# Starting the joined matmul visits at head pair 4 instead of 6, in a linear-attention plus SoLU feed-forward kernel with a written-out instruction order

## The chip, the cores and the metric

The kernel runs on one core of one Trainium2 chip. The metric is the device time of one execution in microseconds (us). A core has five instruction streams that run side by side and meet only at semaphores: TensorE (PE in the profile, its weight loads PEld), VectorE (DVE), ScalarE (ACT), GpSimd (POOL) and SyncE (SP), which here issues every DMA. Each stream is worked off in its own order, so an instruction that waits holds up all that stand behind it on its engine.

## The reference

Attention with a feature map, for 8 batches of 8 heads, 576 tokens and head width 64, and then a feed-forward stage over the 4608 tokens:

```python
proj = x @ w_phi                                   # x is q or k, 64 -> 128
proj = proj - max(abs(proj), axis=-1)
phi  = concat([exp(proj), exp(-proj)])             # 256 features
kv   = k_phi^T @ v ;  z = sum over tokens of k_phi
num  = q_phi @ kv  ;  den = q_phi @ z + 1e-6
x    = num / den                                   # heads side by side: 4608 x 512
h    = x @ w_in                                    # 512 -> 1024
solu = h * softmax(h)
out  = (layernorm(solu) * g_ln) @ w_out            # 1024 -> 512
```

All inputs are float32 (the two big weights arrive as float64 bits and are converted on the chip).

## The kernel before, in words

**Attention.** Heads are handled in pairs. Head pair n (0 to 31) is sub-pair n % 2 of unit u = n // 2, and a unit is half of a batch. For a unit the keys are projected (`kp`, tile `pjk`), reduced to a row maximum (`km`) and subtracted (`ks`, tile `dk`) on VectorE, and exponentiated on ScalarE (`ke`, tile `ek`). The queries go one of two ways. Units 0 to 2 project them like the keys (`qp`, `pjq`; then `dq`), turn them on TensorE (`qT`, tile `dT`) and exponentiate them into the features `fq` (`qe`). From unit 3 on they go through a split into high and low parts (`qh`, `qlo`, tile `hq`), `pq`, VectorE turns (`blk`, `pT`) and two small TensorE turns (`mtp`, `mcp`).

**A visit** (`visit`, line 599; `V` in the plan) is the stretch of matmuls that makes the key-value sums of one pair in one PSUM bank: 10 matmuls `kvT<-ek,...` and then the sums z. For units 0 to 2 (`Z_PE`) the z sums are 20 small matmuls against `ones` and `ones_half`; from unit 3 on they are four matmuls on `zacc`, which GpSimd has added up before.

**From the bank to the query side.** For units 0 and 1 (`KV_PE`) the sums are copied by ScalarE (`kvs`), turned on TensorE (`kvt`) and copied again into `kvf`. From unit 2 on, VectorE turns them (`kve`, tile `kvs`), one DMA takes them to DRAM (`kvo`, `dk<-kvs`) and four DMAs bring them back as `kvf` (`kvi`, `kvf<-dk`). Then `q_num` (line 792) makes two `num` banks out of `fq` and `kvf`, and `q_den` (line 803) one `den` bank. ScalarE empties them (`qv`, `E<-num`; `de`, `dn<-den`), VectorE takes the reciprocal (`dc`, `cmr`), one DMA writes it to DRAM (`ds`, shown as `d<-cmr`), two bring it back over 64 partitions each (`db`, `rb<-d`), and GpSimd multiplies (`dv`, `xa<-E,rb`).

**Joined and separate.** In `visit`, if `before` is set, `q_num` of pair n - 1 stands ahead of pair n's `kvT` matmuls and `q_den` of pair n - 1 behind its z sums. `JOIN` (line 30) is the first pair whose visit does so. For smaller n, `num` and `den` of pair n - 1 are operations of their own (`qo`, `qd`), which may stand anywhere behind their inputs. A joined visit has to wait for the features `fq` and for `kvf` of pair n - 1 at its first matmul, and it takes all three PSUM banks of tag `a`.

**Feed-forward.** The 36 tiles of 128 tokens go through `moe_h` (24 matmuls into the bank pair `h`, of which there is one), a row maximum, exponential, product and turn, a trip through DRAM (`ub`, `du`, `uTs`), a split into `uhs` (ScalarE) and `uls` (GpSimd), and `moe_o` (24 matmuls). The first `moe_h` needs all of the first batch's `dv`, its split `mxh` (ScalarE) and `mxl` (GpSimd), and the four low parts `win_l` of `w_in` (GpSimd), each made from a `win_h` (ScalarE).

**What sets the order.** The function lists some 2620 operations with their engine, tiles and dependences. `SEQUENCE` (line 57) is a written-out order of their numbers, and `Plan.order` follows it: it gives each operation its buffers in that order and emits it, and each engine keeps that order. Every instruction is emitted through the helper `call` of `InOrder`, so all rows of the profile carry that helper's line, L271, and rows are told apart by their tiles.

Of the kernel before, what the change touches and what calls it, by code (L numbers as in the profile page):

```python
# [29 lines left out]
JOIN = 6  # L30
# [27 lines left out]
    99, 3, 2, 88, 0, 132, 126, 7, 136, 102, 4, 100, 101, 90, 103, 104, 5, 127, 107, 95, 89, 91, 230, 130, 14,  # L58
    186, 131, 96, 133, 92, 97, 145, 197, 128, 105, 137, 35, 106, 134, 53, 93, 129, 198, 98, 135, 199, 8, 140,
    109, 108, 138, 94, 148, 9, 142, 114, 149, 118, 143, 139, 146, 224, 147, 110, 115, 41, 10, 116, 150, 15, 111,  # L60
    231, 141, 144, 164, 295, 119, 16, 200, 234, 151, 232, 120, 201, 152, 188, 11, 121, 153, 165, 47, 154, 112,
    202, 187, 17, 113, 203, 156, 193, 36, 233, 155, 194, 166, 189, 157, 117, 225, 37, 158, 204, 18, 54, 170,
    167, 190, 122, 28, 12, 6, 38, 191, 13, 226, 192, 228, 169, 171, 42, 159, 227, 160, 235, 168, 205, 43, 172,
    296, 123, 39, 195, 328, 124, 196, 240, 44, 173, 216, 175, 241, 55, 48, 238, 161, 242, 229, 174, 162, 125,
    45, 29, 297, 285, 56, 246, 217, 243, 247, 218, 30, 248, 207, 245, 49, 244, 219, 31, 249, 46, 176, 50, 250,
    251, 178, 32, 252, 179, 40, 212, 163, 208, 19, 213, 253, 51, 254, 214, 177, 255, 59, 209, 215, 236, 256,
    329, 210, 239, 436, 206, 21, 284, 303, 180, 237, 52, 271, 338, 57, 334, 268, 286, 211, 60, 332, 269, 58,
    262, 287, 220, 257, 263, 437, 330, 61, 288, 264, 331, 22, 291, 270, 333, 272, 298, 438, 221, 181, 289, 62,
    292, 182, 273, 304, 290, 299, 258, 293, 300, 265, 23, 63, 222, 183, 344, 301, 305, 294, 67, 397, 302, 184,
    24, 33, 314, 520, 405, 223, 73, 345, 386, 85, 259, 74, 267, 76, 346, 266, 64, 25, 185, 274, 315, 306, 316,  # L70
    260, 310, 275, 34, 276, 398, 311, 307, 312, 335, 278, 317, 347, 308, 279, 439, 399, 75, 313, 339, 440, 280,
    277, 336, 318, 348, 20, 349, 337, 388, 319, 309, 340, 320, 350, 393, 321, 281, 351, 79, 68, 282, 261, 26,
    387, 389, 500, 352, 341, 394, 27, 390, 353, 441, 468, 354, 372, 442, 355, 511, 77, 342, 356, 283, 373, 395,
    374, 78, 358, 1871, 366, 359, 396, 443, 343, 357, 80, 444, 367, 322, 65, 445, 70, 1892, 446, 391, 82, 360,
    86, 361, 368, 469, 447, 362, 512, 71, 323, 1913, 1872, 81, 1873, 69, 87, 1874, 470, 83, 392, 324, 369, 1875,
    501, 400, 1893, 370, 550, 448, 371, 325, 401, 375, 1876, 449, 326, 1914, 402, 327, 407, 376, 1877, 377, 416,
    471, 408, 1915, 412, 472, 450, 409, 417, 413, 1880, 451, 473, 452, 477, 403, 475, 404, 66, 1916, 474, 1881,
    551, 476, 478, 418, 410, 411, 552, 422, 1917, 479, 1918, 1882, 1883, 1884, 1885, 519, 363, 453, 378, 1919,
    379, 1934, 72, 423, 1922, 1886, 424, 419, 480, 380, 553, 1894, 414, 481, 1923, 554, 364, 454, 425, 482,
    1920, 84, 406, 426, 555, 557, 1878, 427, 483, 1895, 484, 455, 428, 415, 1924, 1887, 457, 1925, 1926, 556,  # L80
    458, 420, 1927, 582, 459, 559, 1896, 1888, 456, 558, 1897, 421, 560, 381, 1898, 365, 382, 429, 1901, 485,
# [12 lines left out]
    1967, 747, 853, 739, 1968, 1969, 635, 608, 1970, 651, 1978, 636, 652, 1971, 637, 640, 638, 683, 641, 653,
    639, 685, 708, 654, 785, 642, 1979, 647, 2028, 709, 686, 684, 687, 643, 710, 1963, 783, 1980, 781, 1972,
    648, 782, 810, 740, 609, 784, 786, 711, 787, 649, 1973, 788, 789, 712, 1981, 713, 1982, 1985, 2029, 655,
    656, 728, 2030, 2031, 741, 2032, 610, 843, 657, 611, 714, 811, 812, 2033, 1986, 688, 612, 1983, 715, 956,
    1953, 2034, 689, 658, 717, 659, 730, 690, 1933, 613, 718, 1987, 742, 731, 2035, 735, 660, 2040, 732, 661,
    736, 662, 733, 743, 663, 734, 744, 1988, 716, 813, 758, 790, 1989, 815, 745, 2041, 892, 814, 737, 791, 816,
    1990, 2025, 738, 719, 792, 746, 759, 819, 793, 817, 2042, 818, 820, 760, 821, 794, 893, 924, 854, 748, 795,  # L100
    691, 1974, 764, 2043, 692, 894, 2044, 720, 693, 1991, 2026, 796, 2045, 722, 721, 723, 749, 799, 724, 694,
    897, 754, 925, 2036, 750, 755, 725, 765, 726, 2048, 1992, 926, 766, 895, 1993, 2049, 1954, 695, 896, 751,
    898, 767, 727, 901, 842, 822, 899, 1912, 823, 1994, 900, 855, 824, 2081, 902, 861, 752, 2082, 903, 768, 753,
    769, 756, 761, 2046, 797, 927, 904, 2083, 757, 800, 905, 928, 801, 906, 762, 798, 907, 825, 2084, 826, 908,
    763, 827, 2085, 2086, 2050, 770, 862, 2051, 2052, 2053, 771, 1984, 828, 2102, 2087, 2123, 2047, 829, 802,
    2054, 772, 803, 2090, 773, 804, 844, 805, 2091, 856, 845, 806, 957, 849, 774, 850, 775, 846, 1070, 857, 847,
    831, 830, 858, 851, 1995, 2124, 909, 2125, 2055, 929, 2126, 848, 852, 872, 832, 931, 2127, 2056, 833, 2088,
    2128, 2092, 776, 2093, 1081, 777, 873, 859, 930, 860, 933, 932, 2057, 2129, 874, 934, 2103, 910, 1006, 2094,
    807, 968, 2095, 1007, 878, 913, 2089, 2037, 2132, 911, 834, 1, 935, 2133, 1975, 835, 912, 1008, 2096, 879,
    880, 863, 836, 2134, 914, 967, 2104, 2058, 1038, 864, 2059, 865, 808, 868, 866, 2038, 881, 869, 867, 882,  # L110
    915, 837, 936, 1011, 1009, 883, 870, 2105, 1010, 884, 871, 1012, 1184, 937, 1997, 2135, 2136, 1013, 2106,
    1015, 2060, 2137, 838, 1014, 2107, 2097, 875, 938, 876, 939, 2098, 877, 1016, 1017, 940, 941, 885, 2130,
    1998, 942, 2138, 2108, 809, 1039, 2061, 916, 917, 1040, 958, 918, 970, 2062, 2139, 2111, 886, 2112, 2109,
    887, 839, 840, 963, 1195, 919, 888, 971, 964, 2113, 959, 889, 965, 972, 2114, 960, 1018, 973, 975, 2063,
    1071, 1019, 961, 945, 1020, 2115, 962, 1082, 943, 1083, 986, 890, 1021, 1047, 2116, 2064, 1041, 920, 2140,
    841, 2065, 944, 2066, 1022, 946, 1023, 2099, 966, 921, 974, 891, 947, 969, 987, 1120, 1042, 1090, 1045,
    1043, 2141, 1044, 1046, 988, 1024, 1048, 1025, 2131, 1049, 2100, 992, 2101, 1121, 2069, 1122, 2070, 2110,
# [1207 lines left out]
```

## Time and profile before

| | us |
|---|---|
| time, median of 3 runs | 709.77 (707.37 to 715.39) |
| the profiled execution, its own time | 708.93 |
| its span, first to last instruction | 707.1 |
| TensorE busy in the span | 694.5 |
| GpSimd busy | 512.3 |
| VectorE busy | 478.1 |
| ScalarE busy | 368.2 |
| first feed-forward matmul | 79.05 after the span's start |
| last matmul begins its operation | 700.00 |

The profiled execution's own time lies 1.8 us over its span, and 0.8 us under the median of the runs. Rows of the timeline give the start, the length, the engine, the line, the tiles written and read, and, in brackets, the idle time before the row and what ended it. On TensorE a row's length runs past the start of the next, since matmuls overlap: what an operation costs there is read from start to start. A float32 matmul leaves two records, so `x16` in a row stands for eight instructions. For DMAs the length is that of issuing on SP; the time to landing is listed apart.

### The profile page before, as it was taken

The page shows a single profiled execution, that of the slowest core. Times are in us where ns is not written, and L with a number is a line of the kernel's source. Part 1 is how long each engine was busy: PE and PEld are TensorE (multiplying, and loading weights), DVE is VectorE, ACT ScalarE, POOL GpSimd, SP SyncE. Part 2 cuts the span into 40 slices and gives each one's busy share as a digit, 9 for nine tenths or more (in the row PEclk, how much of TensorE's full clock was granted, in tenths as well). Part 3 has the DMA queues.
Part 4 walks back from the last instruction along what each step waited for, and adds up shares of the span by engine and source line. Part 5 has one row for each costly group of instructions (what it writes and reads, how often), then busy time and mean ns, then how long its engine had stood idle before and what let it go on. Part 6 is the DMA issues. An engine that isn't in the chain of part 4 may idle for free.

```text
span 707.1 us, 13443 instructions
## 1 busy us (share of the span) xinstructions
PE 694.5 (98%) x4894; PEld 520.2 (74%) x4894; DVE 478.1 (68%) x795; ACT 368.2 (52%) x684; POOL 512.3 (72%) x500
## 2 busy tenths in 40 slices
PE   8999999999999999999999999999999999999997
PEld 6666676777777777777777777777787777788886
DVE  6999787647867668577675777857567775354531
ACT  4997744626545564455554656535554554233231
POOL 1156999997878888789788997978868878361341
PEclk9999999999999999999999999999999999999999
DMA  8954465545575565566545555556374435320331
GB/s 293 339 191 120 114 199 163 157 115 161 162 214 151 143 201 151 166 167 193 144 116 162 188 164 156 173 164 191 107 201 156 127 109 149 94 94 24 124 116 67
DMA packets 113778, 110.04 MB, mean 156 GB/s; under 512 B 57648, under 2 KB 91184, under 8 KB 113200
## 3 DMA queue, kind: packets, MB, share of 16 engines
q1 hardware_dynamic: 113712, 109.18, 51.5%
q8 instruction: 39, 0.64, 0.4%
q14 instruction: 27, 0.22, 0.1%
HBM read 76.75 MB, written 32.39 MB: 154 GB/s over the span
## 4 chain that ended last, share of the span: by engine, by line
PE 64%; POOL 1%; DMA 1%; issue 1%; DVE 1%; ACT 0%; SPq 0%; ACTq 0%; POOLq 0%
PE h L271 22%; PE o L271 22%; PE kvT L271 6%; PE num L271 5%; PE pjk L271 3%; PE pq L271 3%; PE den L271 2%; DMA du<-ub 1%; DMA uTs<-du 0%; POOL xa L271 0%; PE uT L271 0%; PE mcp L271 0%; PE mtp L271 0%; POOL uls L271 0%; POOL zacc L271 0%
## 5 line engine op out<-in xcount | busy, mean ns | idle before, releaser
L271 ACT ACTIVATE ek<-dk 128x512 f32<-128x512 f32 (+1 forms) x160 | 87.2, 583 | 64.5 <-DVE dk L271 64.4
L271 PE MATMUL o<-w_out_h,uhs 128*128 128x512 f32 x264 | 105.3, 399 | 0.0
L271 PE MATMUL o<-w_out_h,uls 128*128 128x512 f32 x264 | 103.3, 391 | 0.1
L271 PE MATMUL o<-w_out_l,uhs 128*128 128x512 f32 x264 | 103.1, 390 | 0.0
L271 POOL TENSOR_TENSOR uls<-uTs,uhs 128x1024 fp32r<-128x1024 f32 x33 | 79.1, 2396 | 25.3 <-ACT uhs L271 22.9
L271 PE MATMUL h<-win_h,mxh 128*128 128x512 f32 x288 | 93.7, 406 | 0.0
L271 PE MATMUL h<-win_l,mxh 128*128 128x512 f32 x288 | 89.5, 392 | 0.0
L271 PE MATMUL h<-win_h,mxl 128*128 128x512 f32 x288 | 89.0, 390 | 0.0
L271 DVE TENSOR_REDUCE nm<-h 128x1 f32<-128x1024 f32 x36 | 43.7, 1215 | 64.5 <-PE h L271 64.4
L271 ACT ACTIVATE fq<-pT 128x576 f32<-128x576 f32 x104 | 68.4, 676 | 20.9 <-DVE pT L271 20.8
L271 POOL TENSOR_TENSOR zt<-ek 128x512 f32<-128x512 f32 x52 | 67.2, 1292 | 15.1 <-ACT ek L271 14.2
L271 POOL TENSOR_TENSOR hq<-rawq,hq 64x1152 fp32r<-64x1152 f32 x26 | 68.9, 2652 | 8.9 <-ACT hq L271 4.2
L271 PE MATMUL num<-fq,kvf 128*64 128x288 f32 x512 | 68.9, 412 | 0.8 <-DMA kvf<-dk 0.5
L271 ACT ACTIVATE eu<-h,nm 128x1024 f32<-128x1024 f32 x36 | 40.2, 1116 | 56.4 <-DVE nm L271 45.8
L271 DVE STREAM_TRANSPOSE blk<-pq 128x288 f32<-128x288 f32 x104 | 45.3, 459 | 28.2 <-PE pq L271 23.7
L271 DVE TENSOR_REDUCE m<-pjk 128x4 f32<-128x512 f32 (+1 forms) x80 | 48.5, 622 | 22.9 <-PE pjk L271 22.7
L271 PEld LDWEIGHTS h<-win_h,mxl 128*128 128x128 f32 x288 | 54.0, 188 | 12.1
L271 PEld LDWEIGHTS h<-win_l,mxh 128*128 128x128 f32 x288 | 54.0, 188 | 12.0
L271 PE MATMUL kvT<-ek,rawv 128*64 128x256 f32 x512 | 61.1, 380 | 0.0
L271 POOL TENSOR_TENSOR blk<-blk,mcol 128x1152 f32<-128x1152 f32 x26 | 55.4, 2131 | 5.7 <-PE h L271 3.5
L271 PEld LDWEIGHTS h<-win_h,mxh 128*128 128x128 f32 x288 | 50.7, 189 | 10.7 <-DVE kvs L271 0.5
L271 PEld LDWEIGHTS o<-w_out_h,uls 128*128 128x128 f32 x264 | 49.5, 188 | 11.5 <-POOL uls L271 0.7
(109 smaller groups left out, 1425.4 us busy)
## 6 DMA issues: line engine op xcount, KB each, us to landing
du<-ub SPq DMA_DIRECT2D x33, 512.0 KB, 2.9
uTs<-du SPq DMA_DIRECT2D x132, 128.0 KB, 3.1
rawq<-in_q SPq DMA_DIRECT2D x26, 576.0 KB, 4.6
rb<-d SPq DMA_DIRECT2D x64, 144.0 KB, 3.3
out<-os SPq DMA_DIRECT2D x35, 256.0 KB, 2.9
rawk<-in_k SPq DMA_DIRECT2D x32, 256.0 KB, 4.5
rawv<-in_v SPq DMA_DIRECT2D x32, 256.0 KB, 3.8
dk<-kvs SPq DMA_DIRECT2D x28, 192.0 KB, 1.9
```

What stands on the lines that cost most here:

```text
L271: return self.tc.keep_in_program_order(method(*args, **kwargs))
```

## The change

`JOIN` becomes 4. So the visits of pairs 4 and 5 (unit 2, sub-pairs 0 and 1) now carry `num` and `den` of pairs 3 and 4. Four operations vanish from the list (`qo` and `qd` of pairs 3 and 4), their 32 matmul instructions move into the two visits, no matmul is added or dropped, and all numbers behind them shift. `SEQUENCE` is a new order throughout, on all five engines. Its table is one line shorter, so the helper's line becomes L270.

```diff
-JOIN = 6
+JOIN = 4
 EARLY = (0, 1, 2)
...
 SEQUENCE = (
-    99, 3, 2, 88, 0, 132, 126, 7, 136, 102, 4, 100, 101, 90, 103, 104, 5, 127, 107, 95, 89, 91, 230, 130, 14,
...
```

Three places of the new order matter below.

TensorE, from the visit of pair 4 to the visit of pair 5. Before: the visit of pair 4, `num` and `den` of pair 3, projections and query turns, then the `kvT` of pair 5.

```order
L271 MATMUL kvT<-ek,ones_half 32x128 x4
L271 MATMUL num<-fq,kvf 64x288 x8
L271 MATMUL den<-fq,kvf 32x288 x8
L271 MATMUL pjq<-wph,rawq_764 128x256
L271 MATMUL dT<-ident,dq 128x128 x3
L271 MATMUL pq<-hq,w_hh 128x288
L271 MATMUL pq<-hq,w_l_76 128x288
L271 MATMUL pjq<-wph,rawq_761 128x128 x8
L271 MATMUL pjk<-wph,rawk 128x128 x8
L271 MATMUL dT<-ident,dq 128x128 x3
L271 MATMUL kvT<-ek,rawv 64x256 x8
```

And now: `den` of pair 3 closes the visit of pair 4, and `num` of pair 4 opens the visit of pair 5.

```order
L270 MATMUL kvT<-ek,ones_half 32x128 x4
L270 MATMUL den<-fq,kvf 32x288 x8
L270 MATMUL dT<-ident,dq 128x128 x3
L270 MATMUL pjq<-wph,rawq_661 128x256
L270 MATMUL pq<-hq,w_hh 128x288
L270 MATMUL pq<-hq,w_l_76 128x288
L270 MATMUL pjk<-wph,rawk 128x128 x8
L270 MATMUL dT<-ident,dq 128x128 x6
L270 MATMUL pjq<-wph,rawq_971 128x128 x8
L270 MATMUL num<-fq,kvf 64x288 x8
L270 MATMUL kvT<-ek,rawv 64x256 x8
```

The `num` of pair 4, which stood behind the `kvT` of pair 5 and more, has moved ahead of them; one more `dT` group stands between the visits, and little else.

SyncE, the round trip of pair 4's sums through DRAM. Before (`d_1041<-cmr` is the reciprocal of pair 3, `kvf<-dk` pair 4's sums coming back, `rb<-d_1041` pair 3's reciprocal coming back):

```order
L271 DMA rb<-d_871 64x2x288
L271 DMA dk<-kvs 128x384
L271 DMA rb<-d_871 64x2x288
L271 DMA vz_73<-in_v 64x128
L271 DMA kvf<-dk 32x12x32
L271 DMA vz_73<-in_v 64x128
L271 DMA d_1041<-cmr 128x9
L271 DMA kvf<-dk 32x12x32 x3
L271 DMA rb<-d_1041 64x2x288 x2
```

And now (`d_1026<-cmr` is that of pair 3):

```order
L270 DMA rb<-d_917 64x2x288
L270 DMA dk<-kvs 128x384
L270 DMA rb<-d_917 64x2x288
L270 DMA d_1026<-cmr 128x9
L270 DMA kvf<-dk 32x12x32 x4
L270 DMA rb<-d_1026 64x2x288 x2
```

All four loads of `kvf` now stand behind the DMA that waits for pair 3's reciprocal; before, one of them stood ahead of it.

ScalarE, from the copy `kvs` of pair 3 to the last features of pair 3. Before:

```order
L271 COPY kvs<-kvT 128x384
L271 ACTIVATE ek<-dk 128x4x128
L271 ACTIVATE fq<-dT 128x288
L271 ACTIVATE ek<-dk 128x4x128 x2
L271 COPY cms<-cmean 128x512
L271 ACTIVATE ek<-dk 128x2x128
L271 ACTIVATE ek<-dk 128x4x128
L271 ACTIVATE ek<-dk 128x2x128
L271 CAST win_h<-w_3_630 128x1024
L271 COPY kvf<-kvt 128x384
L271 ACTIVATE fq<-dT 128x288
L271 CAST w_out_h<-w_5_535 128x512
```

And now, with the last features of pair 3 in the last row:

```order
L270 COPY kvs<-kvT 128x384
L270 ACTIVATE ek<-dk 128x4x128
L270 ACTIVATE fq<-dT 128x288
L270 ACTIVATE ek<-dk 128x4x128
L270 ACTIVATE fq<-dT 128x288 x2
L270 COPY kvf<-kvt 128x384
L270 ACTIVATE ek<-dk 128x2x128
L270 COPY cms<-cmean 128x512
L270 ACTIVATE fq<-dT 128x288
L270 ACTIVATE ek<-dk 128x2x128
L270 ACTIVATE fq<-dT 128x288 x2
```

Before, the last features of pair 3 come in the row behind the last one shown, `fq` x3. Now two `ek` and the casts of `win_h` and `w_out_h` stand elsewhere.

272 rows, old and new, of the table SEQUENCE are left out of this document.

## The prediction

> **What bounds the kernel now.** I read the page first, then the busy times by stage, then TensorE's timeline around the two visits that change, and last the other engines there.
>
> ```profile
> PE 694.5 (98%) x4894; PEld 520.2 (74%) x4894; DVE 478.1 (68%) x795; ACT 368.2 (52%) x684; POOL 512.3 (72%) x500
> PEclk9999999999999999999999999999999999999999
> ```
>
> ```profile
> 20.00:58.45 38.45, 37.21 (x441) 24.55 (x440) 38.17 (x57) 36.96 (x77) 15.69 (x6) 1.00 0.67 226
> 69.00:79.05 10.05, 9.07 (x109) 5.72 (x108) 7.15 (x12) 7.26 (x17) 8.75 (x7) 1.00 0.57 163
> 79.05:120.00 40.95, 40.50 (x279) 29.55 (x278) 33.09 (x54) 22.68 (x44) 40.09 (x30) 1.00 0.52 148
> ```
>
> The columns are stage, length, then PE, PEld, DVE, ACT, POOL busy, clock, DMA share, GB/s. TensorE is the bound, at full clock, and its work is the same after the change. So the time can move only by what TensorE waits or loses between instructions. Up to 58 us VectorE (38.17 of 38.45) and ScalarE (36.96) are as full as TensorE; from 79 to 120 us GpSimd is (40.09 of 40.95). In these stages a delay is not made up easily. The stage that the change rebuilds lies between, from the visit of pair 4 (58.45) to the first feed-forward matmul (79.05). I call the start of pair 4's visit S. From the first feed-forward matmul on, both orders hold the same TensorE work, so what this matmul loses or gains on 79.05 is the forecast.
>
> **The visits themselves.** TensorE now, separate and joined:
>
> ```profile
> 58.45 1.95 PE L271 MATMUL kvT<-ek,rawv 128*64 128x256 f32 x16
> ...
> 60.76 1.08 PE L271 MATMUL kvT<-ek,ones 128*32 128x128 f32 x32
> ...
> 61.99 2.16 PE L271 MATMUL num<-fq,kvf 128*64 128x288 f32 x16
> 64.08 1.18 PE L271 MATMUL den<-fq,kvf 128*32 128x288 f32 x16
> 65.19 0.70 PE L271 MATMUL pjq<-wph,rawq 128*128 128x256 f32 x2
> ...
> 69.00 1.95 PE L271 MATMUL kvT<-ek,rawv 128*64 128x256 f32 x16
> ...
> 72.54 0.55 PE L271 MATMUL dT<-ident,dq 128*128 128x128 f32 x3
> 72.84 0.38 PE L271 MATMUL pq<-hq,w_hh 128*128 128x288 f32 x1
> ...
> 73.20 0.49 PE L271 MATMUL dT<-ident,dq 128*128 128x128 f32 x3
> 73.93 2.16 PE L271 MATMUL num<-fq,kvf 128*64 128x288 f32 x16 [0.25 <-DVE blk L271]
> ...
> 77.56 1.18 PE L271 MATMUL den<-fq,kvf 128*32 128x288 f32 x16 [0.73 <-ACT E L271]
> 78.67 0.41 PE L271 MATMUL pq<-hq,w_hh 128*128 128x288 f32 x1
> ```
>
> ```profile
> 95.18 2.16 PE L271 MATMUL num<-fq,kvf 128*64 128x288 f32 x16
> 97.17 1.90 PE L271 MATMUL kvT<-ek,rawv 128*64 128x256 f32 x16
> ...
> 99.43 0.42 PE L271 MATMUL kvT<-zacc,ones 128*32 128x128 f32 x8
> 99.67 1.15 PE L271 MATMUL den<-fq,kvf 128*32 128x288 f32 x16
> 100.76 0.29 PE L271 MATMUL mtp<-ident,m 128*36 128x128 f32 x1
> ```
>
> Start to start, separate: the visit 58.45 to 61.99 is 3.54, `num` to 64.08 is 2.09, `den` to 65.19 is 1.11, together 6.74. Joined, with the `ones` sums that these two visits keep: `num` 1.99 (95.18 to 97.17), `kvT` 2.26 (97.17 to 99.43), the sums 1.23 (60.76 to 61.99), `den` 1.09 (99.67 to 100.76), together 6.57. Joining saves 0.17 a visit, 0.34 for both. That is the whole direct gain, and it is contained in the absolute times below.
>
> **When pair 4's visit starts (S).** It now waits for pair 3's features. ScalarE before:
>
> ```profile
> 54.31 0.63 ACT L271 ACTIVATE ek<-dk 128x512 f32<-128x512 f32 x1
> 54.84 0.40 ACT L271 ACTIVATE fq<-dT 128x288 f32<-128x288 f32 x1
> ...
> 58.12 1.03 ACT L271 CAST win_h<-w 128x1024 fp32r<-128x1024 f32 x1
> 59.05 0.47 ACT L271 COPY kvf<-kvt 128x384 f32<-128x384 f32 x1
> ...
> 59.72 0.62 ACT L271 CAST w_out_h<-w 128x512 fp32r<-128x512 f32 x1
> 60.23 1.02 ACT L271 ACTIVATE fq<-dT 128x288 f32<-128x288 f32 x3
> ```
>
> The last features ended at 61.25 (60.23 + 1.02), 2.8 after S. The new order takes out from before them two `ek` (0.53 each, 54.31 to 54.84), the `win_h` cast (0.93) and the `w_out_h` cast (0.51), and adds one `fq` (0.30): 61.25 - 1.06 - 0.93 - 0.51 + 0.30 = 59.05. TensorE's own work ahead of S is unchanged, so 58.45 is the lower bound; if nothing of the regrouping helped, 61.25 is the upper. I take S = 59.05, since ScalarE is full up to there.
>
> **The new wait.** `num` of pair 4 had its place at 73.93; now it opens pair 5's visit, which thereby waits for pair 4's `kvf`. SyncE, VectorE and the landing of `kvf<-dk` (55 to 110 us, 12 of them) before:
>
> ```profile
> 67.79 0.33 SPq L271 DMA_DIRECT2D d<-cmr  x1
> 68.17 2.55 SPq L271 DMA_DIRECT2D kvf<-dk  x3
> 70.83 1.27 SPq L271 DMA_DIRECT2D rb<-d  x2
> ```
>
> ```profile
> 66.75 0.22 DVE L271 RECIPROCAL cmr<-dE 128x9 f32<-128x9 f32 x1
> ```
>
> ```profile
> DMA to landing us min/median/max: 2.3/2.9/4.3
> ```
>
> On SyncE all four loads of `kvf` now stand behind `d<-cmr` of pair 3, which waits for pair 3's reciprocal, and that for the `den` at the very end of pair 4's visit. The chain from S: the visit with `den` ends at S + 6.57. From the end of `den` to the end of the reciprocal it took 1.78 (65.19 to 66.97), so S + 8.35. Then `d<-cmr` is issued, 0.38 later the first `kvf<-dk` (67.79 to 68.17), and three more; one took between 0.64 (half of the 1.27 for two, the shape nearest to it) and 0.89 (68.17 to 70.83, three). The last is issued at S + 8.35 + 0.38 + 3 x 0.64 = S + 10.65 and lands 2.9 later: **S + 13.55**. The lower end is a landing of 2.3: S + 12.95. The upper end is the 0.82 that lay between reciprocal and `d<-cmr` before (another DMA stood there), 0.89 an issue and a landing of 4.3: S + 16.5.
>
> TensorE gets to the visit earlier. Between the visits stood 3.81 (65.19 to 69.00); one `dT` group is added, 0.30 (72.54 to 72.84): S + 6.57 + 4.11 = S + 10.7. So TensorE waits about **2.9** (2.3 to 5.8) in front of pair 5's visit, where before it waited 0.25 at `num` and 0.73 at `den`. Queued behind it on TensorE is all that leads to the feed-forward stage; queued on SyncE behind the `kvf` loads are the two `rb<-d` that the first `mxl` needs.
>
> Behind the visit stand three `pq` pairs (0.36 each, 72.84 to 73.20) and two `dT` groups (0.30), 1.7. The first feed-forward matmul then starts at S + 13.55 + 6.57 + 1.7 = S + 21.8 = 80.85 with S = 59.05. That is **1.8 later** than 79.05. Ends: S = 58.45 with the short landing gives 58.45 + 21.2 = 79.65, 0.6 later; S = 59.05 with the long chain 59.05 + 24.8 = 83.85, 4.8 later.
>
> GpSimd has to be ready there too:
>
> ```profile
> 71.48 2.36 POOL L271 TENSOR_TENSOR win_l<-w,win_h 128x1024 fp32r<-128x1024 f32 x1
> 75.15 1.41 POOL L271 TENSOR_TENSOR xa<-E,rb 128x576 f32<-128x576 f32 x1 [1.30 <-DMA rb<-d]
> ...
> 77.75 1.29 POOL L271 TENSOR_TENSOR mxl<-xa,mxh 128x512 fp32r<-128x512 f32 x1
> ```
>
> ```profile
> 76.59 0.62 ACT L271 CAST mxh<-xa 128x512 fp32r<-128x512 f32 x1 [0.84 <-POOL xa L271]
> ```
>
> The `rb<-d` pair is issued behind the `kvf` loads, from S + 11.3; from its first issue to `xa` it took 4.3 (70.83 to 75.15), so `xa` at S + 15.6. A `w_out_l` that filled the 1.2 between `xa` and `mxl` (76.56 to 77.75) stands elsewhere now, but `mxh` on ScalarE still needs its 0.62 there: `mxl` ends 1.41 + 0.7 + 1.29 = 3.4 later, at S + 19.0. In the new order the last `win_l` (2.36) stands behind this `mxl`, not ahead: S + 21.4, 0.4 under TensorE's S + 21.8. So this move costs nothing as long as the wait is there as estimated, and up to its own 2.36 if it is not.
>
> **The sum.** 708.93 (the profiled execution) + 1.8 = 710.7, the saving of 0.34 included. The median of the runs lies 0.84 above that execution, less than their spread of 8; I forecast 710.7.
>
> **The rivals.**
>
> A, *the later start is absorbed by GpSimd's pace*. From 79.05 to 120 GpSimd is at 40.09 of 40.95. If it sets the pace there, its own start counts: `mxl` ends at S + 19.0 = 78.05, 1.0 earlier than the 79.04 (77.75 + 1.29) of before, and then GpSimd has 2.36 more to do (`win_l`) and one `w_out_l` of 1.2 less, so it is 0.2 later in all: 709.1. Against it: TensorE has only 0.45 idle in that stage (40.50 of 40.95), so it can give back little.
>
> B, *the round trip is long* (the slower side). Place: pair 5's visit. Price: wait 5.8, 4.8 later, 713.7. It decides as soon as the last `kvf` lands after S + 13.55, and from there one for one, since nothing else is queued on TensorE that could run. For it: three loads took 2.66 before, and SyncE kept `d<-cmr` for 0.82. Against it: with four loads in a row nothing stands between them.
>
> C, *pair 3's features are not ready earlier*: S = 61.25, the first feed-forward matmul at 83.05, 4.0 later: 712.9. For it: VectorE and ScalarE are full until 58 us. Against it: the four instructions that left are measured.
>
> D, *the clock drops in the long wait*. At the start of the kernel TensorE is slow:
>
> ```profile
> 3.76 3.07 PE L271 MATMUL pjk<-wph,rawk 128*128 128x256 f32 x18
> ...
> 67.53 1.06 PE L271 MATMUL pjk<-wph,rawk 64*128 64x128 f32 x16
> ```
>
> ```profile
> PE pjq L271 <- issue: 1.7, 1, 1.7
> ```
>
> The 18 records took 3.07; the same work later takes little more than half (16 of them 1.06, and two wide ones 0.70 as in the `pjq` row at 65.19). It lasts to 6.8 (3.76 + 3.07); I take 5.6 of it for a second such stretch, as the first matmul of all began about 1 us into the span. If B's wait brought that state back for as long, half of 5.6 would be lost, 2.8: 716.5. The clock row shows full speed throughout, and TensorE's longest wait in this trace is the 1.7 of the row above, so it can't be seen here. The Trainium skill, "TensorE: Matmul & The Clock Gate", section "Part 1: The HAM clock gate", says that the clock is halved after an idle window of about 3.4 us and released after as long a busy one. By that rule the forecast's wait of 2.9 would cost no more than itself, and only B's would set it off; no run here shows that yet.
>
> E, *the new order loses less elsewhere*: TensorE idles 1.24 from 20 to 58.45 and 0.98 from 69 to 79.05, and the new order could fill both with pair 5's wait not showing either: 708.93 - 2.2 - 0.34 = 706.4.
>
> **How the numbers follow.** Forecast 0.50, A 0.20, B 0.12, C 0.08, D 0.04, E 0.06. About 1%, or 7 us, is what a measurement of this kernel tells from no change, since its runs spread by 8. All cases lie within 7 of 709.77. Only D with a late S, or B and C together, pass 716.9: slower by over 1% 0.08. For over 1% faster, TensorE would have to shed 7 us of waits, and the three stages above hold 2.7 of them (1.24, 0.98, 0.45): 0.04. Within 1%: 0.88. The forecast's own range is 709.5 (0.6 later) to 713.7 (4.8 later). The range over the cases reaches from E, less 1.9 for the runs' own scatter (2.4 below the median at the lowest), up to D: 704.5 to 716.5.
>
> **What would show it.** Right: `num` starts pair 5's visit with TensorE idle before it, 2 to 4 us, ended by the DMA `kvf<-dk`; the last `kvf` load issued some 10.7 after pair 4's visit began; the first `h` matmul near 80.9. `d<-cmr` stands idle on SyncE ahead of the loads, and pair 4's visit starts near 59. Wrong: no idle time ahead of pair 5's visit, or one that ends with `fq`; a first `h` before 79; a clock under 1 after it; or a changed idle sum behind 120 us that is larger than all of this.

## The result, and the profile after

The change takes 716.5 us (median of 20 runs, 711.3 to 720.9) where before takes 711.1 in the same session (20 runs, 706.1 to 715.4). The ratio is **1.0076, 95% interval 1.0054 to 1.0098**: slower by three quarters of a per cent, inside the bound of 1%, and 5.4 us where the forecast had 1.8. The profiled execution of the change took 714.81 with a span of 713.0, 5.9 more than before. Two rows of its page, TensorE's busy time and the granted clock:

```profile
PE 696.5 (98%) x4894; PEld 521.7 (73%) x4894; DVE 481.0 (67%) x795; ACT 369.8 (52%) x684; POOL 513.1 (72%) x500
PEclk9999899999999999999999999999999999999999
```

TensorE has the same 4894 records, and one slice of the clock row, the fifth, is no longer full. The three stages of the prediction, cut at this kernel's own marks (start of pair 4's visit, start of pair 5's visit, first feed-forward matmul):

```profile
20.00:61.02 41.02, 37.28 (x434) 24.44 (x432) 40.19 (x57) 37.23 (x81) 18.60 (x7) 1.00 0.62 222
76.01:85.83 9.82, 9.79 (x104) 6.30 (x104) 7.06 (x11) 4.59 (x9) 6.51 (x4) 0.86 0.22 84
85.83:120.00 34.17, 33.68 (x212) 25.03 (x214) 28.63 (x47) 20.07 (x41) 32.77 (x26) 1.00 0.60 179
```

Up to pair 4's visit TensorE is idle for 3.7 us (41.02 - 37.28), where it was 1.2; around pair 5's visit it has almost no idle time, but a clock of 0.86. TensorE's timeline shows where:

```profile
56.51 0.67 PE L270 MATMUL pjk<-wph,rawk 128*128 128x256 f32 x2 [2.13 <-issue]
...
61.02 2.16 PE L270 MATMUL num<-fq,kvf 128*64 128x288 f32 x16
...
67.47 0.55 PE L270 MATMUL dT<-ident,dq 128*128 128x128 f32 x3
...
70.65 0.33 PE L270 MATMUL dT<-ident,dq 128*128 128x128 f32 x1 [0.31 <-DVE dq L270]
72.07 0.87 PE L270 MATMUL dT<-ident,dq 128*128 128x128 f32 x3 [1.08 <-DVE dk L270]
72.87 2.08 PE L270 MATMUL pjq<-wph,rawq 64*128 64x128 f32 x16
76.01 3.49 PE L270 MATMUL num<-fq,kvf 128*64 128x288 f32 x16 [1.06 <-DMA kvf<-dk]
...
83.78 0.40 PE L270 MATMUL pq<-hq,w_hh 128*128 128x288 f32 x1
...
85.83 0.73 PE L270 MATMUL h<-win_h,mxh 128*128 128x512 f32 x2
```

The first `h` comes at 85.83, 6.8 later than the 79.05 of before; 0.9 of it is given back by the end. In order: 2.13 idle in front of `pjk`, so that pair 4's visit starts at 61.02 (S); a joined visit of 6.45 (61.02 to 67.47); three gaps of 0.31, 1.08 and 1.06; 16 `pjq` records in 2.08, and a `num` of 3.49 where the same 16 took 2.16 at 61.02. Three windows of 3.41, 6.83 and 3.41 us say why these two are slow:

```profile
68.50:71.91 3.41, 2.17 (x21) 1.48 (x19) 3.34 (x9) 2.76 (x7) 3.41 (x3) 1.00 0.30 77
71.91:78.74 6.83, 5.62 (x31) 3.94 (x33) 6.72 (x11) 1.11 (x4) 1.90 (x2) 0.50 0.71 197
78.74:82.15 3.41, 3.41 (x46) 2.27 (x46) 2.86 (x3) 2.27 (x5) 2.68 (x3) 1.00 0.02 6
```

The clock is exactly 0.50 from 71.91 to 78.74. The loads of pair 4's `kvf` on SyncE:

```profile
67.25 0.33 SPq L270 DMA_DIRECT2D dk<-kvs  x1
67.62 0.58 SPq L270 DMA_DIRECT2D rb<-d  x1
69.05 0.33 SPq L270 DMA_DIRECT2D d<-cmr  x1
69.49 2.64 SPq L270 DMA_DIRECT2D kvf<-dk  x4
```

The last of the four is issued at 71.50, S + 10.48, and lands 4.4 later; pair 5's visit starts at 76.01, S + 14.99. The row of `pjk` says `<-issue` for its 2.13 us: the profile shows nothing that ended them. I put them down to VectorE, which was late with everything behind the following instruction (its row, then GpSimd's up to 51 us and from there); the experiments test that:

```profile
48.58 3.44 DVE L270 SCALAR_TENSOR_TENSOR w<-wraw,w 128x1024 uint32<-128x1024 uint32 x1
```

```profile
48.56 2.37 POOL L270 TENSOR_TENSOR wsum<-wsum,w 128x1024 f32<-128x1024 f32 x1
...
51.01 3.25 POOL L270 TENSOR_TENSOR wsum<-wsum,w 128x1024 f32<-128x1024 f32 x1
```

I call this third bit step of `w`'s tile 0 **the bit step**. Alone it takes 1.22. Here it started 0.02 after a `wsum`, and ended at 52.02, 1.09 after that `wsum` ended (50.93): it did not run beside it, it waited for it. The next `wsum` in turn took 3.25 in place of 2.37.

### The profile page after: what moved, and what is told of

Same layout as the page of the kernel before. It is cut to its first block, busy times and chain, and to the rows that moved or that the text cites. A ratio compares the mean times of both kernels' runs of the same rounds, so it can differ in the third digit from the quotient of the medians.

```text
span 713.0 us, 13426 instructions
## 1 busy us (share of the span) xinstructions
PE 696.5 (98%) x4894; PEld 521.7 (73%) x4894; DVE 481.0 (67%) x795; ACT 369.8 (52%) x684; POOL 513.1 (72%) x500
## 4 chain that ended last, share of the span: by engine, by line
PE 80%; DVE 7%; DMA 5%; SPq 3%; issue 2%; ACT 2%; POOL 0%; ACTq 0%; DVEq 0%; POOLq 0%
PE h L270 26%; PE o L270 24%; PE kvT L270 9%; PE num L270 7%; PE pjk L270 5%; PE pq L270 3%; PE den L270 3%; SPq L270 3%; DVE w L270 2%; DVE m L270 2%; DMA uTs<-du 1%; DMA rawq<-in_q 1%; DVE dk L270 1%; DMA d<-cmr 1%; DVE eu L270 1%
## 5 line engine op out<-in xcount | busy, mean ns | idle before, releaser
L270 ACT ACTIVATE ek<-dk 128x512 f32<-128x512 f32 (+1 forms) x160 | 86.9, 582 | 51.9 <-DVE dk L270 51.8
L270 POOL TENSOR_TENSOR uls<-uTs,uhs 128x1024 fp32r<-128x1024 f32 x33 | 78.9, 2392 | 40.3 <-ACT uhs L270 35.6
L270 PE MATMUL o<-w_out_h,uhs 128*128 128x512 f32 x264 | 105.0, 398 | 0.0
L270 PE MATMUL o<-w_out_h,uls 128*128 128x512 f32 x264 | 103.2, 391 | 0.0
L270 PE MATMUL o<-w_out_l,uhs 128*128 128x512 f32 x264 | 103.1, 390 | 0.0
L270 PE MATMUL h<-win_h,mxh 128*128 128x512 f32 x288 | 94.0, 407 | 0.5 <-DVE eu L270 0.5
L270 PE MATMUL h<-win_l,mxh 128*128 128x512 f32 x288 | 89.5, 392 | 0.0
L270 PE MATMUL h<-win_h,mxl 128*128 128x512 f32 x288 | 89.1, 390 | 0.0
L270 POOL TENSOR_TENSOR zt<-ek 128x512 f32<-128x512 f32 x52 | 67.3, 1294 | 16.1 <-ACT ek L270 12.3
L270 ACT ACTIVATE fq<-pT 128x576 f32<-128x576 f32 x104 | 68.0, 678 | 17.7 <-DVE pT L270 16.8
L270 POOL TENSOR_TENSOR hq<-rawq,hq 64x1152 fp32r<-64x1152 f32 x26 | 69.0, 2655 | 8.6 <-ACT hq L270 3.2
L270 DVE TENSOR_REDUCE nm<-h 128x1 f32<-128x1024 f32 x36 | 43.6, 1210 | 44.8 <-PE h L270 44.6
L270 PE MATMUL num<-fq,kvf 128*64 128x288 f32 x512 | 70.6, 419 | 1.1 <-DMA kvf<-dk 1.1
L270 DVE STREAM_TRANSPOSE blk<-pq 128x288 f32<-128x288 f32 x104 | 45.1, 460 | 35.9 <-PE pq L270 32.3
L270 DVE TENSOR_REDUCE m<-pjk 128x4 f32<-128x512 f32 (+1 forms) x80 | 48.6, 620 | 28.0 <-PE pjk L270 27.9
L270 ACT ACTIVATE eu<-h,nm 128x1024 f32<-128x1024 f32 x36 | 40.2, 1117 | 46.2 <-DVE nm L270 42.2
L270 PEld LDWEIGHTS h<-win_h,mxl 128*128 128x128 f32 x288 | 54.1, 188 | 12.2
L270 PEld LDWEIGHTS h<-win_l,mxh 128*128 128x128 f32 x288 | 54.0, 188 | 12.1
L270 PE MATMUL kvT<-ek,rawv 128*64 128x256 f32 x512 | 60.9, 380 | 0.0
L270 PEld LDWEIGHTS h<-win_h,mxh 128*128 128x128 f32 x288 | 50.5, 189 | 11.2 <-issue 1.1
L270 DVE STREAM_TRANSPOSE pT<-blk 128x288 f32<-128x288 f32 x104 | 41.7, 444 | 24.3 <-POOL blk L270 21.1
L270 PEld LDWEIGHTS o<-w_out_h,uls 128*128 128x128 f32 x264 | 49.5, 188 | 11.0 <-POOL uls L270 0.2
```

What stands on the lines that cost most here:

```text
L270: return self.tc.keep_in_program_order(method(*args, **kwargs))
```

## The experiments

**The theory** after this reading has three causes: VectorE held up by GpSimd ahead of pair 4's visit (2.1 us), the round trip of `kvf` with what stands in its queue (the forecast's own), and the clock (1.3 us). **The rivals**: the time is the price of joining alone; or it is the price of the new order alone. Ratios below are to before on the same chip in the same session. Their intervals are some 0.2% wide on each side, so two kernels are told apart only from 0.3% on, about 2 us. Each kernel left one profile, and the same program can differ by 1.5 us from one profile to the next (the change's two, below), so a time read from a single trace is no finer than that.

### The loads ahead of `d<-cmr` (e1_loads_first)

```diff
 SyncE
-d<-cmr (pair 3)
 kvf<-dk (pair 4) x4
+d<-cmr (pair 3)
 rb<-d (pair 3) x2
```

> The change with one move: on SyncE d<-cmr of pair 3 stands behind the four kvf<-dk of pair 4 instead of ahead of them. Theory of the prediction (the loads queue behind d<-cmr, which waits for the end of den): the loads start as soon as kvf's own data are in DRAM. If that was much earlier, the wait in front of pair 5's visit shrinks by over 1 us. Rival (the round trip by itself is as long): dk<-kvs was issued at 67.25 and a load can't start before it has landed, about 2 us later, which is where the first load stood anyway (69.49); then pair 5's visit starts at most 0.4 us earlier (75.6 in place of 76.01) and the time falls by 0 to 0.4 us. I expect the rival: 716.1 to 716.5, clock still dropping to 0.5 near 72.

Ratio 1.0059 (1.0035 to 1.0082). SyncE, then TensorE:

```profile
68.32 0.33 SPq L269 DMA_DIRECT2D dk<-kvs  x1
68.69 0.58 SPq L269 DMA_DIRECT2D rb<-d  x1
70.22 2.63 SPq L269 DMA_DIRECT2D kvf<-dk  x4
```

```profile
75.96 2.37 PE L269 MATMUL num<-fq,kvf 128*64 128x288 f32 x16
...
84.62 0.40 PE L269 MATMUL pq<-hq,w_hh 128*128 128x288 f32 x1 [1.20 <-ACT dn L269]
```

The first load comes 1.90 after `dk<-kvs` where it came 2.24 after: standing behind `d<-cmr` cost 0.34, because the load could not start much earlier anyway. Two chains, over the reciprocal and over `dk`, end almost together. Pair 5's visit no longer waits (no load took 4.4 here) and starts at S + 13.87, 1.1 earlier where I expected at most 0.4; 1.20 turn up at once at a `pq` behind it.

### The bit step elsewhere (e2_w_later), three places later (e13_three_places)

```diff
 VectorE (e2; the load of raw tile 2 and its rescaling move behind it too)
-w<-wraw,w (tile 0, third step)
 m<-pjq (pair 4)
 ...
 cmr<-dE
+w<-wraw,w (tile 0, third step)
 w<-w,cms (wc 3)
```

> The change with the third bit step of w of tile 0 (the VectorE instruction that took 3.44 in place of 1.22 beside GpSimd's wsum) moved behind the second reciprocal, where GpSimd is idle; the load of raw tile 2 and its rescaling move behind it. Theory (VectorE was held up by GpSimd there, and all of VectorE behind it was late): it takes 1.22 again, wsum takes 2.4 both times, TensorE's 2.13 idle in front of pjk at 56.5 is gone, pair 4's visit starts at 58.6 to 59.4 in place of 61.02, the first h about 2 us earlier (83.5 to 84.3), and the time is 714.0 to 715.0. Rival (pair 3's features are late because ScalarE is full, whatever VectorE does): the visit starts at 60.5 or later, time 716 to 716.5.

```diff
 VectorE (e13; the load of raw tile 2 moves behind it too)
-w<-wraw,w (tile 0, third step)
 m<-pjq
 m<-pjk
 m<-pjq
+w<-wraw,w (tile 0, third step)
```

> The change with one thing alone: the bit step of w stands three places later on VectorE (behind two row maxima more and the one of pair 4's q), with the load that waits for it. Theory (a two-operand VectorE instruction that starts while GpSimd's wsum runs waits for the end of that wsum, and no longer): it starts at about 50.6, 0.3 before the wsum ends, and takes 1.2 to 1.6 in place of 3.44; TensorE's idle of 2.1 in front of pjk is under 0.6; pair 4's visit starts 1.6 to 2.3 earlier against (2,qp,0), the time falls by 1 to 2.6 us. Rival (the instruction is slow beside GpSimd wherever it stands): it takes over 2.5, time unchanged.

e2: ratio 1.0040 (1.0018 to 1.0061). TensorE's idle in front of `pjk` is gone, and pair 4's visit starts 11.30 behind the start of the first `pjq` of pairs 4 and 5 in place of 13.57, 2.27 earlier. But the bit step still took 2.75, now beside a `win_l`; and behind pair 5's visit a new idle stands. VectorE, GpSimd and TensorE of e2:

```profile
58.20 2.75 DVE L269 SCALAR_TENSOR_TENSOR w<-wraw,w 128x1024 uint32<-128x1024 uint32 x1
...
78.31 4.56 DVE L269 TENSOR_TENSOR w<-w,cms 128x512 f32<-128x512 f32 x2
```

```profile
57.51 2.36 POOL L269 TENSOR_TENSOR win_l<-w,win_h 128x1024 fp32r<-128x1024 f32 x1
...
78.04 1.50 POOL L269 TENSOR_TENSOR mxl<-xa,mxh 128x512 fp32r<-128x512 f32 x1 [0.73 <-ACT mxh L269]
79.58 2.73 POOL L269 TENSOR_TENSOR win_l<-w,win_h 128x1024 fp32r<-128x1024 f32 x1
```

```profile
83.92 1.54 PE L269 MATMUL dT<-ident,dq 128*128 128x128 f32 x6 [2.51 <-DVE blk L269]
```

The bit step ends at 60.95, 1.08 after the `win_l` (59.87). The two centrings of `w_out` (`w<-w,cms`, its column mean subtracted), 0.68 each alone, took 4.56 beside `mxl` and the next `win_l`, and the row subtraction and the `blk` in front of this `dT` stand behind them. The first `h` came at 85.11, but this whole trace runs 1.3 us later than the change's before the two orders part. Counted from the start of pair 3's visit (50.29 in the change, 51.60 here), it came after 33.5 in place of 35.5: 2.0 earlier. The ratio, 0.36% lower than the change's, says the same, 2.5 us, just over what can be told apart.

e13: ratio 1.0091 (1.0057 to 1.0124). The bit step started at 50.70, and the next `wsum` had started at 50.57:

```profile
50.70 3.32 DVE L269 SCALAR_TENSOR_TENSOR w<-wraw,w 128x1024 uint32<-128x1024 uint32 x1
```

```profile
50.57 2.37 POOL L269 TENSOR_TENSOR wsum<-wsum,w 128x1024 f32<-128x1024 f32 x1
```

My 1.2 to 1.6 missed, since I had not counted on the next `wsum` standing right behind. It ends 1.08 after that one (52.94), as an instruction does that waits for the other. The length of 3.32 alone would not tell this from a fixed slowness. What does is another bit step, some 30 us later, which started beside an `xa` in e3, e4, e5, e11, e13 and e14: it took anything from 1.42 to 2.32, and always ended 1.08 to 1.09 after that `xa`. The idle in front of `pjk` was 2.77, and nothing was gained.

### TensorE kept busy in the gaps (e3_keep_busy)

```diff
+def keep_busy(n):
+    t = bank("kv", [P, 512], "keep")
+    for _ in range(n):
+        nc.tensor.matmul(t[:, :P], lhsT=ident, rhs=ident, start=True, stop=True)
 TensorE
 pjk (pair 6)
+keep_busy(1)
 dT (pair 4)
+keep_busy(5)
 dT (pair 4)
 pjq (pair 5)
+keep_busy(5)
 the visit of pair 5
```

> The change with 11 matmuls more on TensorE, whose results nobody reads: 1, 5 and 5 of 128x128 on the identity, put where TensorE idled 0.31, 1.08 and 1.06 us between pair 4's and pair 5's visits. The wait for kvf stays. Theory (those gaps made the clock drop to 0.5 from 71.9 to 78.7, which cost pair 5's visit 7.77 - 6.45 = 1.3): the granted clock stays 1.00, the visit takes 6.45, the first h comes about 1.3 earlier (84.5), time 715.0 to 715.4. Rival (the clock drops for another reason, such as the small matmuls of the visits): clock 0.5 again, time as the change, 716.5 to 717.

Ratio 1.0056 (1.0028 to 1.0083), 0.20% or 1.4 us under the change, as expected, though the interval does not resolve it alone. Its windows from the gaps to the end of pair 5's visit, and TensorE behind it:

```profile
68.90:77.03 8.13, 8.09 (x83) 6.47 (x75) 7.71 (x15) 4.73 (x11) 5.09 (x4) 1.00 0.36 89
77.03:83.55 6.52, 6.52 (x94) 4.07 (x93) 6.52 (x7) 2.68 (x5) 3.59 (x3) 1.00 0.57 166
```

```profile
87.20 0.91 PE L269 MATMUL dT<-ident,dq 128*128 128x128 f32 x6 [2.59 <-DVE blk L269]
```

The clock stays full there and the visit takes 6.45, so it was the gaps that lowered it in the change. They don't always: the same two gaps stand in e2 and e13, where the clock stayed full. And this profile is not free of half clock either, with 3.41 us of it at 9.61, at 57.40 (behind the 2.12 idle in front of `pjk`) and at 88.12 (behind the 2.59 shown here).

The runs give an estimate of the price. From a run's mean clock and span follows, rounded, how many times 3.41 us it ran at half clock, (1 - clock) x span / (0.5 x 3.41). Of the 34 runs of before that stood beside e1 to e4, 2 had none (mean 708.4), 10 one (709.7) and 22 two (711.1): about 1.35 us each. Seven of the experiments' profiles show one or two of them between 9 and 18 us, far ahead of the visits. The change had two to four in 19 of 20 runs, 2.7 in the mean of these; the twentieth, 720.9 us, had a mean clock of 0.943. e3 had 1.8. The profiled execution of before, on which the forecast stood, was one with none.

### Joined and apart (e4_pair5_apart, e5_both_apart, e6_old_order)

```diff
-joined = n >= JOIN
+joined = n >= JOIN and n not in (5,)
 ...
-joined = JOIN <= n + 1 < 4 * B
+joined = JOIN <= n + 1 < 4 * B and n + 1 not in (5,)
 TensorE
 the visit of pair 5
+num, den (pair 4)
```

> The new order with only pair 4's visit joined: pair 5's key-value sums stand alone in the same place, and pair 4's numerators and denominators behind them. Theory (joining pair 5's visit put 3.5 us of sums that need no kvf behind the wait for kvf): the sums start when TensorE gets there, 74 to 75, num starts near 77.6 without a wait over 0.3, den ends near 80.8 in place of 83.8, the clock stays 1.00, the first h starts when mxl is there (82.2 to 82.8), 3 us earlier than in the change; time 713.2 to 714.0. Rival (GpSimd, which sets the pace from 79 to 120 us, takes the gain back): first h earlier, but the time stays within 1 us of the change, 715.5 to 716.5.

e5 has (4, 5) there, and pair 3's `num` and `den` behind pair 4's visit.

> The new order without either of the two new joins: pair 4's and pair 5's key-value sums stand alone where their joined visits stood, with the numerators and denominators of the pair before right behind. Rival of the prediction (the new order itself is what costs, by VectorE instructions that stall beside GpSimd's, and joining is nearly free): the time stays within 1 us of the change with pair 5 apart, 712 to 713.5, with TensorE's idle before pjk near 56 and the late first h (85 or later) both still there. The prediction's theory (the wait that joining adds is the price): 2 to 3 us faster than the change with one join, 709.5 to 710.5.

```diff
 TensorE, in the order of before
-kvT (pair 4's visit)
-num, den (pair 3)
+num (pair 3), kvT (pair 4), den (pair 3): one visit
 ...
-kvT (pair 5's visit)
 ...
-num, then den (pair 4)
+num (pair 4), kvT (pair 5), den (pair 4): one visit
+dT (pair 5, moved from ahead of it)
 ScalarE, in the order of before
+ek, E<-num (pair 4)
 fq (pair 5)
-ek
 fq (pair 5)
-E<-num (pair 4)
```

> The order of before with the two joins put into it: pair 4's visit moves to where pair 3's numerators stood, pair 5's to where pair 4's numerators stood, with one turn of pair 5's q behind it; nothing else is moved. Theory of the prediction (a joined visit waits for the features and for kvf): pair 4's visit waits for pair 3's features and starts near 61.3 in place of 58.45, the kvf chain of pair 4 ends some 13.5 after that, 74.8, and the first h comes at about 83, 4 later than before: 713.5 to 715. Rival (joining is nearly free, the order costs): within 1.5 us of before, 709.5 to 712.

e4: 1.0034 (1.0011 to 1.0057). e5: 1.0041 (1.0012 to 1.0071). e6: 1.0138 (1.0110 to 1.0165). Without any new join the new order is still slower than before, with an interval that excludes no difference: **about half of the loss, 0.41 of 0.76%, is there without joining**. Taking one or both joins out of it gains 0.35 to 0.42%, just about what can be told apart. That is not a clean price of the joins. e5's profile, as shown below, is also without the stall of the bit step, and e2, which has both joins and no idle in front of `pjk`, stands at 1.0040, where e5 stands. Neither rival holds alone. In e6 two instructions moved on ScalarE as well (diff above). It lost 9.8 us where I expected 4 to 5: in its trace pair 4's visit waits 1.06 for pair 3's `kvf` and, in the middle of its `num`, 1.03 for `fq`, and 1.75 and 2.32 follow ahead of a `pjq` and a `dT`. In e4's trace the sums started near the expected 74 to 75:

```profile
75.10 2.94 PE L269 MATMUL kvT<-ek,rawv 128*64 128x256 f32 x16
...
79.63 2.16 PE L269 MATMUL num<-fq,kvf 128*64 128x288 f32 x16
```

But they did not fill a wait: the last `kvf` load, issued at 72.36, had landed at 74.65, before they began. So what e4 gains is not that wait. The clock had dropped here too (2.94 for what takes 1.90), and the first `h` came at 85.41, not at 82.2 to 82.8. What settles the bit step is e5, where it and the `wsum` stand as in the change:

```profile
48.74 1.22 DVE L269 SCALAR_TENSOR_TENSOR w<-wraw,w 128x1024 uint32<-128x1024 uint32 x1
```

```profile
48.72 3.46 POOL L269 TENSOR_TENSOR wsum<-wsum,w 128x1024 f32<-128x1024 f32 x1
```

```profile
54.44 0.67 PE L269 MATMUL pjk<-wph,rawk 128*128 128x256 f32 x2
...
58.95 1.30 PE L269 MATMUL kvT<-ek,rawv 128*64 128x256 f32 x10
```

```profile
58.28 0.75 ACT L269 ACTIVATE fq<-dT 128x288 f32<-128x288 f32 x2
```

The same two instructions, started within 0.02 us of each other, went the other way: the `wsum` waited (3.46), the bit step took 1.22, TensorE has no idle in front of `pjk`, pair 4's visit starts at 58.95, and pair 3's features end at 59.03 (58.28 + 0.75) in place of 61.10. All traces of the new order agree. Counted from the start of pair 3's visit, pair 4's starts after 8.45 to 8.50 in the six without that idle (e2, e5, e9, e10, e11, e12), joined or apart. With it, it starts after 10.70 to 10.73 (e1 and the change), 11.36 (e13), and 12.27 to 12.37 (e3, e4, e14), where the idle time fell into one of the 3.41 us stretches and the next one ran at half clock. The Trainium skill, "SBUF — State Buffer", section "Who interferes with whom", says that a VectorE instruction with two inputs in SBUF and a GpSimd instruction that reads SBUF exclude each other, and that the one issued first blocks the other until it has finished. The traces agree that they exclude each other: in nine of them (change, e1, e2, e3, e4, e9, e10, e13, e14) the bit step ended 1.08 to 1.09 after the GpSimd instruction that was ahead of it. Which of the two was issued first they do not show: by its row the `wsum` starts 0.02 ahead in the change and in e5 alike.

### The change again (e14_change_again)

> The change once more, unchanged, beside the others on the same chip. If the stall of the bit step is decided by which of two instructions starts first (wsum at 48.56, the bit step at 48.58), either 3.4 or 1.2 may stand in this profile; if it is 1.2, TensorE's idle in front of pjk is gone with it. The landing of the last kvf load, 4.4 in the first profile, should be 2.3 to 3.2 as in the other kernels, and then pair 5's visit does not wait for it. Time 715.5 to 717.5 where before is at 711.

Ratio 1.0076 again (1.0045 to 1.0108). TensorE:

```profile
74.07 0.52 PE L270 MATMUL dT<-ident,dq 128*128 128x128 f32 x3 [1.08 <-DVE dk L270]
...
76.14 3.26 PE L270 MATMUL num<-fq,kvf 128*64 128x288 f32 x16
...
86.82 0.91 PE L270 MATMUL dT<-ident,dq 128*128 128x128 f32 x6 [2.00 <-DVE blk L270]
```

The stall of the bit step is there again (3.42), and the 1.08 in front of `dT`. The wait for `kvf` is not: the last load, issued at 73.50, landed 2.2 later, at 75.73. The 1.06 of the first profile was one slow landing (4.4). Pair 5's visit starts at S + 13.13. S itself is 1.5 later than in the first profile, counted from pair 3's visit: the clock was at 0.50 from 57.92 to 61.33, behind the idle time in front of `pjk`, where in the first profile it stayed full.

### Moves together (e9_three_moves, e10_three_moves_apart, e11_w_work_early, e12_and_reciprocal_later)

```diff
 e9: e1's and e2's moves, and on VectorE
-w<-w,cms (wc 1 and 5, behind the bit steps of tile 2)
 ...
 m<-blk (pair 6's q)
+w<-w,cms (wc 1 and 5; their casts on ScalarE follow)
```

> The change, both visits joined, with three moves: the kvf loads ahead of d<-cmr, the bit step of w behind the second reciprocal, and the two centrings of w_out (wc 1 and 5) that stalled beside mxl and win_l moved behind the row maximum of pair 6's q. Theory (each single move was eaten by the next VectorE instruction that GpSimd holds up): no TensorE idle over 0.6 ahead of dT after pair 5's visit, first h at 81.5 to 82.8, 3 us earlier than with the bit step moved alone, time 709.5 to 711. Rival (GpSimd's pace from 79 to 120 us takes it back): first h earlier, but time 712.5 to 713.5 as with one move.

> The same three moves with both visits apart. What it differs by from the kernel with three moves is the joining alone. If joining saves what the sum says (0.17 a visit) and its waits are hidden, this one is 0 to 0.5 us slower; if the joined visits still wait for features or kvf, this one is 1 to 3 us faster.

e9: 1.0073 (1.0047 to 1.0099), e10: 1.0100 (1.0076 to 1.0123). My move was at fault: by the buffers of the order, `mxl` of the second token tile takes the one that these centrings read until 88.80. GpSimd and TensorE of e9:

```profile
88.94 1.30 POOL L269 TENSOR_TENSOR mxl<-xa,mxh 128x512 fp32r<-128x512 f32 x1 [3.28 <-ACT w_out_h L269]
```

```profile
94.58 0.43 PE L269 MATMUL mcp<-ident,mb 128*128 128x128 f32 x1 [2.96 <-POOL mb L269]
```

As a pair they still tell what joining does when nothing else differs: apart is 0.27% slower, not resolved, with the sign of the saving.

```diff
 e11: e2's moves, and
 VectorE
 dk<-pjk,m (pair 4)
+w<-w,cms (wc 4, 0, 1, 5; from behind 73 us)
 kvs<-kvT (pair 4)
 GpSimd
-win_l (tile 3, at 57 us)
 xa (pair 1)
+win_l (tile 3)
 e12: e11, and
 VectorE
-cmr<-dE (pair 3)
 dq<-pjq,m (pair 4)
+cmr<-dE (pair 3)
 SyncE: the loads ahead of d<-cmr, as in e1
```

> The change with the bit step of w moved as before, the four centrings wc 4, 0, 1, 5 moved ahead of pair 4's kve (61 to 65 us), and GpSimd's win_l of tile 3 moved out of that stretch to where GpSimd idles (72 us). So VectorE's two-operand work on w stands where GpSimd does little, and no buffer is held longer. Theory (VectorE's stalls beside GpSimd are what ate each gain): no VectorE instruction on w over 1.9 us behind 70, no TensorE idle over 0.6 ahead of dT after pair 5's visit, first h 20.9 to 21.8 us after pair 4's visit began, where the change took 24.8; time 709.5 to 711.5, ratio 0.998 to 1.002. Rival (GpSimd's pace takes it back later, or a new wait): ratio 1.004 or more, as with the bit step alone.

> The kernel before with two moves more: on VectorE pair 3's reciprocal, which waits for the end of pair 4's visit, stands behind the row subtraction that TensorE's dT waits for; on SyncE d<-cmr stands behind the four kvf loads. Theory (what stands behind den on an engine waits with it): TensorE's idle of 1.1 in front of dT is under 0.3, the granted clock stays 1.00 between the two visits, pair 5's visit starts 12.4 to 13.2 after pair 4's (13.8 without the moves), and the time falls by another 0.3 to 1.5 us. Rival: rb and with it mxl come later by about 2 us and take it back: no change or up to 1 us slower.

e11: 1.0065 (1.0042 to 1.0088), e12: 1.0073 (1.0046 to 1.0100), both misses. Up to 61 us they have the same order. VectorE's four centrings, e11 then e12, and GpSimd's `xa` beside them:

```profile
60.93 2.48 DVE L269 TENSOR_TENSOR w<-w,cms 128x512 f32<-128x512 f32 x4
```

```profile
60.99 3.70 POOL L269 TENSOR_TENSOR xa<-E,rb 128x576 f32<-128x576 f32 x1 [5.52 <-DMA rb<-d]
```

```profile
60.98 7.97 DVE L269 TENSOR_TENSOR w<-w,cms 128x512 f32<-128x512 f32 x4
```

```profile
60.85 1.40 POOL L269 TENSOR_TENSOR xa<-E,rb 128x576 f32<-128x576 f32 x1 [5.34 <-DMA rb<-d]
```

In e11 VectorE was 0.06 ahead and `xa` waited for all four (3.70); in e12 `xa` was 0.13 ahead, and then the two engines took turns, 7.97 for the same four. In e11 pair 4's visit started at 58.13, without the idle time in front of `pjk`, but pair 5's at S + 16.4: pair 3's `dn` on ScalarE now stood behind the copies of `E`, which waited for that `xa`'s buffer, and behind two casts of the moved work. In e12 `kvs<-kvT` stood behind the centrings and came 5.1 later than in e11 (68.88 for 63.74), so its own question, the reciprocal, was not tried.

## Why the prediction was right or wrong

**Right: faster, same or slower.** It gave 0.88 to no difference over 1%, and the interval lies inside that bound, on the slower side as forecast. That the time is still covered is owed to the width of the range and not to the sum: 716.5 is its upper edge, and the 5.4 us between the medians are three times the 1.8. Two of the prediction's own signs of being wrong came, a clock under 1, and, in e14, no idle time ahead of pair 5's visit.

**Right: the joined visit.** 6.45 against 6.57. **Right: the chain to the last load**, S + 10.48 and S + 10.49 in two profiles against S + 10.65. Its reason was half wrong: by e1, `d<-cmr` costs 0.34 of it; the rest is the round trip of `dk` itself.

**Wrong: "I take S = 59.05, since ScalarE is full up to there".** It was 61.02. ScalarE's sum was right (the features ended at 59.03 in e5, where VectorE was not held up), but the term had no VectorE in it. By its number this is rival C (61.25, a chance of 0.08), by its cause not: C assumed that the new order saves ScalarE nothing. It saved what the sum says, and VectorE delayed what ScalarE works on. I had moved ScalarE's instructions and not asked what the new order puts beside what on VectorE and GpSimd. It puts the bit step, which before stood at 20 us with GpSimd idle, next to the `wsum`.

**Wrong: "TensorE gets to the visit earlier ... S + 10.7".** It got there at S + 13.93 (74.95) and S + 13.13. The forecast named what queues behind `den` on SyncE and left out VectorE, where the reciprocal waits for `den` too. Behind it stand the `dq` that the first `dT` needs (0.31) and the `dk` that frees the second one's bank (1.08, in ten of the traces). In each of the ten VectorE had stood idle for `dn` ahead of that reciprocal, 0.25 to 2.82; that it is the reciprocal which makes them late is read from this and from the order, and was not tried. e5 and e10, which have no new join, are among the ten, so these gaps come with the order and not with joining. The half clock from 71.91, with 2.08 for `pjq`, is in the S + 13.93 too.

**Wrong: the wait for `kvf`, "about 2.9".** It was 1.06 in the change, behind the one landing of 4.4, 0.39 in e2, 0.84 in e13, and none in the other six profiles of the new order with pair 5's visit joined (e1, e3, e9, e11, e12, e14): TensorE came so late that the loads were there. That the three gaps of the first profile make 2.45 (0.31 + 1.08 + 1.06) is near 2.9 by chance. The visit started at S + 14.99 in the first profile and S + 13.13 in e14, against S + 13.55.

**Wrong: rival D, "the clock drops in the long wait", 0.04.** It happened, at 71.91, without a long wait: in the ten us before it no gap was over 1.1. The rule that I weighed there, one idle window of 3.4, does not hold for this trace: the window from 68.50 to 71.91 was busy for 2.17 of 3.41 and the next one was at half clock. Its price is an estimate, 1.35 for each such stretch by the runs of before; e3's 1.4 is within the noise.

**Wrong: the basis.** 708.93 was a profile without a stretch at half clock, which only 2 of those 34 runs of before have.

By terms: the forecast's 1.8, the bit step's 2.1 and the clock's 1.4 make 5.3, and the medians lie 5.4 apart. That is arithmetic and not shown. For the bit step it nearly is: e2 took the idle time in front of `pjk` away, and 2.5 us of the loss went with it, although a new VectorE stall of 2.51 stands further back. e3's 1.4 is not resolved, with a stall of 2.59 in the same place. For the 1.8, the price of joining, the runs show none: with that idle time gone, joined and apart are level (e2 1.0040, e5 1.0041), or joined is ahead by an unresolved 0.27% (e9 and e10). What makes the other half of the loss, the 0.4% that e2 and e5 keep, stays open, and with it whether an order exists in which the two joins pay; the kernels tried here give none that beats before.

## What to carry to other kernels

When an order is changed, list for every VectorE instruction with two SBUF inputs which GpSimd instruction runs beside it, before and after: the two wait for each other, and when their starts lie 0.02 us apart the order does not tell which one waits. When something is queued behind a late result, look for every engine that waits for that result, not for the one that the change is about. And a TensorE that idles in pieces of about 1 us can pay a second time, by a lower clock in the 3.4 us that follow.

## What the runs showed of the hardware

- The bit step took 1.22 (e5), 2.75 (e2), 3.32 (e13) or 3.44 (change), by what GpSimd was doing beside it. A row of four such instructions on VectorE held one GpSimd instruction for their whole length in e11 (`xa` 3.70 in place of 1.41), and in e12, where `xa` started 0.13 ahead, was drawn out from 2.48 to 7.97.
- Where TensorE's clock dropped, it was 0.50 for 3.41 us or a multiple of it (6.83, and 10.24 in e12), in every trace but that of before. The Trainium skill, "TensorE: Matmul & The Clock Gate", section "Part 1: The HAM clock gate", gives a free-running window of 3413 ns, and the lengths agree. A wholly idle window was not needed: drops out of full clock followed windows with 1.11 (e11, from 67.19) to 2.98 us (e13, from 82.16) of idle time. Idle time alone does not decide, since other windows kept the clock with up to 1.86 (e13, from 54.84).
